# A new list of tasks, engines and addresses for four interleaved state-space and long-convolution layers on one core

## The chip, the cores and the metric

The kernel runs on one core of a Trainium2 chip. Time is device microseconds (us) of one execution of the whole program. Its engines are PE (matrix products; PEld is its weight load), DVE (vector), ACT (scalar functions), POOL (GpSimd) and SP (SyncE, which here only issues DMAs; SPq in the trace).

## What is computed

The input x has 2048 tokens of 640 channels. Two kinds of layer alternate, A, B, A, B, each added to x after a normalisation:

```python
x = x + _A_ref(_layernorm(x), Lambda_re, Lambda_im, B_re, B_im, C_re, C_im, log_dt, Dskip)
x = x + _B_ref(_layernorm(x), k, v, shift_k, ssm_k, ssm_D)
x = x + _A_ref(...)
x = x + _B_ref(...)
# _A_ref: Lam_bar = exp(dt*Lam); h[t] = Lam_bar*h[t-1] + x[t] @ B_bar.T   (complex, 640 states)
#         y = 2*Re(h @ C.T) + x*Dskip
# _B_ref: kv = conv4(k, shift_k) * v;  y = causal_conv(kv, ssm_k) + kv*ssm_D;  return q*y   (q is the normalised x)
```

Both A layers share their weights, and both B layers share y, which doesn't depend on x.

## The kernel before, in words

The work is cut into 912 named tasks. Each is added with S.add(name, engine, estimate, dependencies, function), and S.run (class Sched, L203) emits them in the order of one list of names, ORDER (L54). A name with /a, /d or /p chooses ACT, DVE or POOL for a task that may run on more than one. Each engine and SP's queue run their own tasks in the order of the list, and an engine stops at the first one whose inputs, buffer or PSUM bank are not ready. PLACE (L121) gives each buffer its address in one SBUF tile (arena, units of 64 bytes) or its PSUM bank (banks). The estimates and xt, a transfer time given to S.add for DMAs, are stored in the task and read by nothing in this program. Two buffers whose places overlap make the later one's first writer wait for the earlier one's last reader.

The tasks, by their names (N is a block of 128 channels, 0 to 4; c a chunk of 512 tokens, 0 to 3):

- yt_*: tables of sines and cosines for the transform in y (yt_sin on ACT, L857 to 859; yt_Ci and yt_Si are transposed copies by DMA, L872; yt_nsi, L876, writes the table NSi).
- kv_*N: kv_lkN loads k transposed (L1031), kv_lvN loads v (L1039), kv_mmN multiplies on PE (L1052), kv_evN multiplies by v on DVE (L1058). kv_dsN and kv_pdN prepare operands.
- a_*: weights of the A layers. a_ldB loads B, a_wl0j:c loads C transposed (L409, ten DMAs), a_wc (ACT, L413) and a_wm (DVE, L417) scale it, a_b0, a_b1 and a_w1 are products with copies a_b0e, a_b1e, a_w1e behind them, a_t2 ends the tables.
- yqN_*: the long convolution y of block N as a two-step transform. yqN_kl (L1133) loads ssm_k, yqN_vl (L1151) transposes kv from SBUF to SBUF by DMA. KA, KB, VA and VB (matmuls :m L1088, L1112 to 1117; copies out of PSUM :e, L254 on ACT or L256 on DVE) transform both, yqN_pw (L1165 to 1168) multiplies on DVE, IB (L1187, 1188) goes back, yqN_tt (L1200) transposes by DMA, IA (L1215) ends it and yqN_st (L1225) stores y in DRAM (ysd).
- xlc loads x, A1cc_xr loads it once more for the residual (L1313, L1317).
- Layers A1 and A2, chunk c: statistics (_ln_bn, L572, or _ln_sq, L545), _id (normalise), _tu (transpose by DMA, L629), _bq (L648) and _bp (L663, L665) on PE with copies _eq and _ev, then on DVE _ri (L680, 681, 684), the scan _sc (L692 to 697), the carry _cy (L708 to 710), _ro and _hx (L722), and on PE _cp:q (L745), with _xe:q (L753 on ACT, L755 or L757 on DVE) writing the new x and its sums.
- Layers B1 and B2, chunk c: B1lc, B2lc load y (L1328; they wait for all stores yqN_st), statistics, _u (normalise, L599 on ACT, L601 on DVE), _mm (L802), _m (L808 or L810). The last chunk of B2 goes token by token (_u L787, _m L791), and _st stores the output (L773).

The chain of one chunk is thus xl, _ln, _id, _tu, _bq, _bp, _ri, _sc, _ro, _hx, _cp, _xe, then B1 with y, then A2 and B2 in the same way. The scan of chunk c+1 waits for the carry of chunk c.

Of the kernel before, what the change touches and what calls it, by code (L numbers as in the profile page):

```python
# [66 lines left out]
    yq1_VA:m2 kv_mm2:0 kv_lv3 yq0_IB:e3/a a_wm04:0 yq1_VA:e2/a yq0_IB:m1 kv_ev2:0 a_wc02:0 yq0_IB:m4 yq1_VA:m1 a_wc04:1 yq0_IB:e1/d yq2_kl yq0_IB:m2
    yq1_VA:e1/a yq1_KB:m4 a_wm00:0 yq0_IB:e2/a yq1_VB:m1 a_wm02:0 yq0_IB:e4/a a_wl03:1 yq1_KB:e4/d a_wc00:1 yq1_VB:m0 a_wm04:1 yq1_VB:e1/a kv_mm3:0 yq2_vl
    a_wm00:1 yq1_VB:e0/a yq1_VB:m3 kv_ev3:0 a_wc02:1 yq1_VB:m2 yq1_VB:e3/a yq2_ka a_wm02:1 a_wl03:0 yq2_KA:m3 yq2_KA:m0 yq2_KA:e3/a kv_mm3:1 yq2_KA:e0/d
    yq0_tt yq1_VB:e2/a yq1_VB:m4 kv_ev3:1 yq2_KA:m2 yq1_VB:e4/a yq2_KA:m1 yq2_KA:e2/a yq1_pw yq2_VA:m3 yq2_KA:e1/a yq2_VA:m0 yq2_VA:e3/a yq2_KB:m2  # L70
    yq2_VA:e0/a yq2_VA:m2 kv_lv4 yq2_KB:e2/a yq2_KB:m0 yq2_VA:e2/a yq2_KB:m1 yq2_KB:e0/a xl0 yq0_IA:m0 a_wc03:0 kv_mm4:1 yq0_IA:e0/a a_wm03:0 yq2_KB:e1/a
    yq3_vl yq1_IB:m3 kv_ev4:1 a_wc03:1 yq2_KB:m4 yq1_IB:m4 yq1_IB:m2 yq2_KB:e4/a yq1_IB:e3/a a_wm03:1 yq1_IB:m1 yq3_kl A1c0_ln_bn:2/d yq1_IB:e4/a
    yq1_IB:e2/a yq0_IA:m1 yq2_VA:m1 A1c0_ln_bn:3/d yq1_IB:e1/a kv_mm4:0 A1c0_ln_bn:1/d yq0_IA:e1/a xl2 yq1_IB:m0 yq2_VA:e1/a A1c0_ln_bn:0/d yq2_KB:m3
    yq1_IB:e0/a kv_ev4:0 yq2_VB:m1 A1c0_ln_sd yq1_tt yq2_VB:m3 yq2_KB:e3/d yq2_VB:m0 yq2_VB:e1/a A1c0_ln_post yq2_VB:m2 yq3_ka yq2_VB:e0/d yq2_VB:e3/a
    yq3_KA:m3 yq2_VB:e2/a A1c0_id:0/d yq2_VB:m4 A1c0_id:3/d yq2_VB:e4/d A1c0_id:2/a yq3_KA:m2 yq2_pw yq3_KA:m1 A1c0_id:1/a yq3_KA:e3/a A1c0_tu yq3_KA:e1/a
    yq3_KA:e2/a yq3_KA:m0 yq3_KA:e0/a yq1_IA:m0 xl1 yq1_IA:m1 yq1_IA:e0/a yq3_KB:m1 yq1_IA:e1/a yq3_KB:m3 yq4_kl yq3_KB:e1/a yq3_VA:m3 A1c2_ln_bn:0/d
    yq2_IB:m3 yq3_VA:e3/a yq3_KB:e3/d yq2_IB:m2 yq2_IB:e3/a yq2_IB:m1 yq1_st A1c2_ln_bn:2/d yq2_IB:e2/a yq3_VA:m2 yq2_IB:m0 yq2_IB:e1/d yq3_VA:e2/a
    yq2_IB:m4 yq3_KB:m4 A1c2_ln_bn:3/d yq2_IB:e0/a yq0_st yq3_VA:m1 yq3_KB:m0 yq3_VA:e1/a yq2_IB:e4/d A1c0_bq:2 A1c2_ln_bn:1/d yq3_KB:e4/a yq3_KB:e0/a
    yq3_KB:m2 yq4_ka yq2_tt A1c1_ln_bn:2/d A1c0_eq:2/a yq3_VA:m0 yq4_KA:m0 A1c1_ln_bn:3/d A1c0_bp:2 yq3_VA:e0/a yq3_KB:e2/d A1c2_ln_sd yq3_VB:m2
    A1c0_ev:2/a A1c2_ln_post yq4_KA:e0/a A1c0_bq:1 A1c1_ln_bn:1/d yq3_VB:e2/a A1c2_id:0/d A1c1_ln_bn:0/d yq4_KA:m3 yq3_VB:m0 A1c2_id:2/d A1c0_eq:1/a  # L80
    yq4_KA:e3/d yq3_VB:m1 yq3_VB:e0/a A1c2_id:1/d yq3_VB:m4 yq3_VB:m3 A1c2_id:3/d A1c1_ln_sd yq3_VB:e4/d A1c2_tu A1c1_ln_post yq4_KA:m2 A1c0_bp:1
    yq3_VB:e3/a A1c1_id:3/d yq4_KA:e2/d yq3_VB:e1/a yq3_pw yq4_KA:m1 A1c0_bq:0 A1c0_ev:1/a xl3 yq4_KA:e1/a yq2_IA:m1 A1c0_xr A1c0_eq:0/a A1c2_bq:2
    yq2_IA:m0 A1c2_eq:2/a A1c0_bp:0 yq4_vl yq2_IA:e0/a yq2_IA:e1/a A1c1_id:0/a A1c1_id:1/d yq3_IB:m1 A1c1_id:2/d A1c0_ev:0/d A1c1_tu A1c2_bp:2 yq3_IB:e1/a
    A1c0_ri yq3_IB:m2 A1c2_ev:2/a yq3_IB:m3 yq3_IB:e2/a yq2_st yq3_IB:m0 yq3_IB:e3/a yq4_KB:m2 yq3_IB:e0/a yq4_KB:m3 yq4_KB:e2/a A1c0_sc A1c1_bq:0
    yq4_KB:e3/a A1c1_bq:1 A1c1_eq:0/a yq4_KB:m1 A1c1_eq:1/a A1c0_cy yq4_KB:m4 A1c0_ro A1c1_bq:2 yq4_KB:e1/a yq4_KB:m0 yq3_IB:m4 A1c1_bp:0 yq3_IB:e4/a
    yq4_KB:e0/a A1c3_ln_bn:3/a yq4_KB:e4/d yq3_tt A1c1_eq:2/d A1c2_bq:0 A1c3_ln_bn:1/d A1c1_ev:0/d yq4_VA:m3 A1c1_bp:2 A1c2_eq:0/a yq4_VA:e3/d yq4_VA:m0
    A1c3_ln_bn:2/d yq4_VA:m2 A1c1_bp:1 yq4_VA:e0/a A1c3_ln_bn:0/d A1c1_ev:2/a yq4_VA:e2/a A1c0_hx A1c3_ln_sd yq4_VA:m1 A1c2_bp:0 yq4_VA:e1/d A1c1_ev:1/d
    A1c3_ln_post yq4_VB:m3 A1c1_ri A1c2_bq:1 yq4_VB:e3/a A1c2_ev:0/a yq3_IA:m1 A1c2_eq:1/a yq4_VB:m4 yq4_VB:m2 yq4_VB:e4/a yq3_IA:e1/a A1c2_bp:1 A1c1_sc
    A1c1_xr yq4_VB:e2/a a_w10:4 A1c2_ev:1/a yq4_VB:m0 yq4_VB:m1 A1c0_cp:3 yq4_VB:e1/a yq4_VB:e0/d a_w1e0:4/a yq4_pw a_w10:1 A1c0_xe:3/a a_w10:3 a_w1e0:1/a
    a_w11:0 a_w1e0:3/a a_w10:0 a_w10:2 a_w1e1:0/a a_w11:2 a_w1e0:0/a a_w11:3 a_w1e0:2/a a_w11:4 a_w1e1:2/a a_w11:1 a_w1e1:4/a A1c0_cp:1 a_w1e1:3/a  # L90
# [191 lines left out]
def a_setup_tasks(S, nc, wp, St, consts, A_Lambda_re, A_Lambda_im, A_B_re, A_B_im, A_C_re, A_C_im, A_log_dt, A_Dskip, after_sin):  # L282
# [111 lines left out]
    t_bl = []  # L394
# [209 lines left out]
class ALayer:  # L604
# [6 lines left out]
    def chunk(self, c, src, sums_in, x_ready, resid, s_x, sums_out, s_src, reload):  # L611
        S, nc, aw, AT = self.S, self.nc, self.aw, self.AT
        small = self.small
        nm = f"{self.lname}c{c}"
# [5 lines left out]
        outs = []  # L620
# [750 lines left out]
```

## Time and profile before

| | us |
|---|---|
| median of 4 runs (lowest to highest) | 351.93 (350.55 to 354.01) |
| the profiled execution: its own time | 351.71 |
| its span, first to last instruction | 349.7 |
| DMA: moved in all | 41.70 MB in 111276 packets |

Spans in the trace start at its first instruction, so an event "at 130.67" is that far into the 349.7 us. A line of the time line gives start, length, engine, line of the code, operation, what it writes <- reads, the number of instructions merged, and in brackets how long the engine had been idle and what ended that. A "work ahead" of a task is the sum over one engine's tasks in front of it in the list, each from its start to the next one's start, less the idle time: what the engine has to do before it, without waits. The time at which the trace has the task, less its work ahead, is how long the engine had been idle by then.

### The profile page before, as it was taken

The numbers are of one execution on the slowest core, as the hardware profiler recorded it, in microseconds if no ns is written. First come the engines' busy times: TensorE is split into PE (matmuls) and PEld (weight loads), VectorE is DVE, ScalarE is ACT, GpSimd is POOL, SyncE is SP. The second block draws the span as 40 slices with busy tenths as digits, with TensorE's granted clock in tenths as the row PEclk, the third lists the DMA queues.
The fourth block names the chain that finished last, engine by engine and source line by source line (L and its number), as shares of the span: only waits on it lengthen the run. The fifth ranks groups of instructions, "written<-read, shape, count | busy, mean of one in ns | idle before, by whom it ended". The sixth has DMA issues, their size and how long they took to land.

```text
span 349.7 us, 9369 instructions
## 1 busy us (share of the span) xinstructions
PE 309.8 (89%) x4060; PEld 248.6 (71%) x4060; DVE 327.7 (94%) x455; ACT 254.6 (73%) x405; POOL 22.3 (6%) x58
## 2 busy tenths in 40 slices
PE   7687989779599989999999999999999999899900
PEld 7576878679598889896676786776877787566500
DVE  8999989988989999899999699999999999999996
ACT  5999999979997775655867669985975874007760
POOL 6567000000000000000000000000000000000000
PEclk9789999989899999999999999999999999999965
DMA  8999999999995990601049921703217400000033
GB/s 237 185 150 200 191 166 195 185 219 192 182 257 107 227 187 3 120 9 69 2 99 196 292 108 30 200 10 67 75 32 197 75 3 1 2 0 2 16 134 150
DMA packets 111276, 41.70 MB, mean 119 GB/s; under 512 B 104830, under 2 KB 106115, under 8 KB 111235
## 3 DMA queue, kind: packets, MB, share of 16 engines
q1 hardware_dynamic: 111088, 41.10, 57.2%
q8 instruction: 31, 0.51, 0.6%
q14 instruction: 11, 0.08, 0.1%
q10 hardware_dynamic: 146, 0.01, 0.0%
HBM read 17.38 MB, written 5.24 MB: 65 GB/s over the span
## 4 chain that ended last, share of the span: by engine, by line
PE 54%; DVE 27%; DMA 8%; ACT 7%; issue 2%; POOL 0%; DVEq 0%; POOLq 0%; ACTq 0%; SPq 0%
PE banks L745 18%; PE banks L663 10%; PE banks L648 9%; DMA arena<-arena 8%; DVE arena L697 5%; ACT arena L254 5%; DVE arena L680 4%; DVE arena L256 3%; DVE arena L757 2%; DVE arena L681 2%; DVE arena L810 2%; PE banks L1187 2%; PE banks L1188 2%; PE banks L665 2%; PE banks L1112 2%
## 5 line engine op out<-in xcount | busy, mean ns | idle before, releaser
L254 ACT ACTIVATE arena<-banks 128x1024 bf16<-128x1024 f32 (+3 forms) x150 | 129.1, 927 | 37.5 <-PE banks L665 10.3
L745 PE MATMUL banks<-arena 128*128 128x128 bf16 (+1 forms) x800 | 100.9, 283 | 1.3 <-DVE arena L681 1.3
L745 PEld LDWEIGHTS <-arena 128*128 128x128 bf16 x800 | 60.5, 98 | 41.3 <-DVE arena L681 1.4
L663 PE MATMUL banks<-arena 128*128 128x256 bf16 x400 | 53.3, 273 | 0.0
L648 PE MATMUL banks<-arena 128*128 128x256 bf16 x400 | 46.0, 273 | 1.2 <-ACT arena L254 1.2
L680 DVE TENSOR_TENSOR arena<-arena 128x5160 bf16<-128x5160 bf16 x16 | 45.5, 2842 | 0.3
L256 DVE CAST arena<-banks 128x1024 bf16<-128x1024 f32 (+4 forms) x43 | 41.7, 981 | 4.0 <-issue 1.2
L697 DVE TENSOR_TENSOR_SCAN arena<-arena 128x1290 bf16<-128x1290 f32 x16 | 44.7, 2833 | 0.3
L648 PEld LDWEIGHTS <-arena 128*128 128x128 bf16 x400 | 38.5, 98 | 5.7 <-DMA arena<-arena 1.4
L663 PEld LDWEIGHTS <-arena 128*128 128x128 bf16 x400 | 38.5, 98 | 4.8
L545 ACT ACTIVATE junk<-arena,nmean 128x640 bf16<-128x640 f32 x48 | 39.6, 825 | 1.1
L599 ACT ACTIVATE arena<-arena,nmr,rstd 128x640 bf16<-128x640 f32 (+1 forms) x37 | 32.5, 914 | 8.7 <-DVE nmr L558 8.5
L1112 PE MATMUL banks<-arena 128*128 128x128 bf16 x170 | 36.1, 225 | 1.4 <-ACT arena L254 0.9
L1115 PE MATMUL banks<-arena 128*128 128x128 bf16 x170 | 36.4, 224 | 0.0
L1114 PE MATMUL banks<-arena 128*128 128x128 bf16 x150 | 33.6, 224 | 0.0
L1117 PE MATMUL banks<-arena 128*128 128x128 bf16 x150 | 33.4, 223 | 0.0
L681 DVE TENSOR_TENSOR arena<-arena 128x2580 bf16<-128x2580 bf16 x16 | 24.1, 1503 | 0.6
L665 PE MATMUL banks<-arena,ident_bf 128*128 128x256 bf16 x80 | 21.8, 272 | 0.0
L540 ACT ACTIVATE nmean<-sums 128x4 f32<-128x4 f32 (+1 forms) x15 | 3.0, 199 | 24.7 <-DVE arena L757 17.8
L1187 PE MATMUL banks<-arena 128*128 128x128 bf16 x160 | 20.8, 227 | 0.2 <-ACT arena L254 0.2
L1188 PE MATMUL banks<-arena 128*128 128x128 bf16 x160 | 20.7, 227 | 0.0
L1088 PEld LDWEIGHTS <-arena 64*128 64x128 bf16 x320 | 10.1, 97 | 11.9 <-issue 7.1
(195 smaller groups left out, 508.5 us busy)
## 6 DMA issues: line engine op xcount, KB each, us to landing
arena<-in_A_x_dram SPq DMA_DIRECT2D x8, 640.0 KB, 6.8
arena<-ysd SPq DMA_DIRECT2D x8, 640.0 KB, 5.2
arena<-in_B_ssm_k_dram SPq DMA_DIRECT2D x5, 512.0 KB
arena<-in_B_v_dram SPq DMA_DIRECT2D x5, 512.0 KB, 4.9
ysd<-arena SPq DMA_DIRECT2D x5, 512.0 KB, 6.8
out_dram<-arena SPq DMA_DIRECT2D x8, 320.0 KB, 2.2
arena<-in_A_B_re_dram SPq DMA_DIRECT2D x1, 800.0 KB, 4.8
arena<-in_A_B_im_dram SPq DMA_DIRECT2D x1, 800.0 KB, 6.6
```

The source lines that it names most:

```text
L254: nc.scalar.activation(out, in_, ACT.Copy)
L256: nc.vector.tensor_copy(out, in_)
L545: nc.scalar.activation(small.junk, src(q), ACT.Square, bias=st["nmean"][:, i:i + 1], scale=1.0, accum_out=st["ssq"][:, i:i + 1])
L648: nc.tensor.matmul(pq[:, jj, c2, :], lhsT=bt0[:, c2, k, j * P:(j + 1) * P], rhs=uT[:, 2:4, k, :], start=(k == 0), stop=(k == NJ - 1))
L663: nc.tensor.matmul(pb[:, jj, c2, :], lhsT=bt1[:, c2, j, k, :], rhs=uT[:, 0:2, k, :], start=(k == 0), stop=False)
L680: nc.vector.tensor_tensor(tt, gs[:, :, None].to_broadcast([P, 2, 2, n]), by_pairs(w["tab"].get().rearrange("p i j b -> p (i j b)"), n), AL ...
L697: nc.vector.tensor_tensor_scan(gv, rt, gv, 0.0, ALU.mult, ALU.add)
L745: nc.tensor.matmul(pc[:, o0:o1], lhsT=lh, rhs=rh, start=(n == 0), stop=(n == len(ops) - 1))
L1112: nc.tensor.matmul(ps[:, g, 0, :], lhsT=T["Cf"].get()[:, q, :], rhs=are, start=True, stop=single)
L1114: nc.tensor.matmul(ps[:, g, 0, :], lhsT=T["Sf"].get()[:, q, :], rhs=A[:, 2 * q + 1, :], start=False, stop=True)
L1115: nc.tensor.matmul(ps[:, g, 1, :], lhsT=T["NSf"].get()[:, q, :], rhs=are, start=True, stop=single)
L1117: nc.tensor.matmul(ps[:, g, 1, :], lhsT=T["Cf"].get()[:, q, :], rhs=A[:, 2 * q + 1, :], start=False, stop=True)
```

## The change

ORDER and PLACE are replaced as a whole; both hold the same 912 tasks and the same buffers. 67 tasks with a choice change between ACT and DVE (34 to DVE, 33 to ACT) and five between DVE and POOL. The order changes on every engine, by less than 20 places of the list for most tasks; further go, among others, yq2_kl and yq2_ka (112 places earlier), yq4_vl (73 earlier), yq1_vl (58 earlier), kv_lk3 (78 later), kv_lk4 (62 later), yq1_st (135 later), yq2_st (47 later), A1c0_xr (75 later), a_wl02:1 (156 later), B2l1 (145 earlier). Besides, some of the xt numbers are new. Some of its lines (ORDER and PLACE have 64 and 42 lines on each side):

```diff
 ORDER = """
...
-    yq1_VA:m2 kv_mm2:0 kv_lv3 yq0_IB:e3/a a_wm04:0 yq1_VA:e2/a yq0_IB:m1 kv_ev2:0 a_wc02:0 yq0_IB:m4 yq1_VA:m1 a_wc04:1 yq0_IB:e1/d yq2_kl yq0_IB:m2
...
-    yq3_VB:e3/a A1c1_id:3/d yq4_KA:e2/d yq3_VB:e1/a yq3_pw yq4_KA:m1 A1c0_bq:0 A1c0_ev:1/a xl3 yq4_KA:e1/a yq2_IA:m1 A1c0_xr A1c0_eq:0/a A1c2_bq:2
-    yq2_IA:m0 A1c2_eq:2/a A1c0_bp:0 yq4_vl yq2_IA:e0/a yq2_IA:e1/a A1c1_id:0/a A1c1_id:1/d yq3_IB:m1 A1c1_id:2/d A1c0_ev:0/d A1c1_tu A1c2_bp:2 yq3_IB:e1/a
...
-    a_w1e1:1/a A1c3_id:1/d A1c3_id:3/a A1c1_cy A1c1_ro yq4_IB:m3 yq3_IA:m0 yq4_IB:e3/a A1c0_cp:0 yq3_IA:e0/a A1c3_id:0/a A1c0_xe:1/d yq3_st A1c2_ri
...
+    yq0_vl kv_mm1:0 kv_ev1:1 yq0_KB:m3 kv_ev1:0 a_b01:1 yq0_KB:m4 yq2_kl a_lamd a_b01:0 yq0_KB:e4/a a_b0e1:1/a yq0_KB:e3/d yq1_vl a_b10:1 a_b0e1:0/a
...
+    yq1_VA:m3 kv_mm2:1 yq1_VA:e3/a yt_nsi a_wl03:0 yq1_VA:e0/a a_wm00:0 yq0_IB:m3 a_wl04:1 kv_ev2:1 a_b1e1:1/a yq0_IB:m0 a_wc02:0 kv_mm2:0 kv_lk3 a_t2
+    yq0_IB:e3/a yq0_IB:e0/d yq1_VA:m2 kv_ev2:0 yq1_VA:e2/a yq0_IB:m1 kv_lv3 a_wc04:0 yq0_IB:m4 yq1_VA:m1 yq0_IB:m2 yq0_IB:e4/d yq1_VA:e1/a yq0_IB:e1/d
...
+    yq3_KB:e1/a A1c2_ln_bn:3/d yq2_IB:m3 yq3_VA:e3/a yq3_KB:e3/d yq2_IB:m2 yq2_IB:e3/a yq2_IB:m1 A1c2_ln_bn:1/d yq2_IB:e2/a yq4_vl yq3_VA:m2 yq2_IB:m0
...
+    yq2_IA:m0 A1c1_tu A1c0_eq:0/a yq4_KB:m4 yq2_IA:m1 A1c2_bq:2 yq2_IA:e0/a A1c3_ln_bn:3/a A1c0_bp:0 A1c2_eq:2/d yq4_KB:e4/d yq2_IA:e1/d A1c2_bp:2
...
+    A1c1_hx yq4_IB:m3 yq4_IB:e1/a yq4_IB:m0 yq4_IB:e3/d yq4_IB:m2 yq4_IB:e0/a yq4_IB:m4 A1c0_cp:2 yq4_IB:e2/a yq4_IB:e4/d A1c2_ri yq4_tt A1c1_cp:3
...
 PLACE = {
...
-    3176, "x2:2": 1565, "x2:3": 444, "A1c2_u": 288, "A1c2_uT": 2326, "A1c2_g": 1284, "A1c2_q": 524, "A1c2_t": 1565, "A1c2_t2": 1571, "xb3": 2429, "xr3":
...
+    "x2:1": 3038, "x2:2": 40, "x2:3": 2638, "A1c2_u": 507, "A1c2_uT": 2326, "A1c2_g": 1284, "A1c2_q": 524, "A1c2_t": 873, "A1c2_t2": 1571, "xb3": 2406,
...
-        t_bl.append(S.add(f"a_ldB{i}", "sp", 0.5, [], e_ld, xt=2.2, uses=[s_B[i]]))
+        t_bl.append(S.add(f"a_ldB{i}", "sp", 0.5, [], e_ld, xt=2.6, uses=[s_B[i]]))
...
-        H["t_tt"] = S.add(f"yq{qd}_tt", "sp", 4.9, eI, e_tt, xt=5.5, uses=[s_TT, s_T])
+        H["t_tt"] = S.add(f"yq{qd}_tt", "sp", 4.9, eI, e_tt, xt=4.4, uses=[s_TT, s_T])
```

The other new xt numbers are those of a_wl (0.95 to 1.2), _tu (3.3 to 3.4), kv_lk (2.7 to 2.5), kv_lv (2.4 to 2.7), yqN_vl (2.6 to 2.75) and yqN_st (2.2 to 1.9).

## The prediction

> **What bounds the kernel now.** I read the page's busy shares first, then the busy time by stage, then the chain that ended last, and last the time line of the engines around each wait.
>
> ```profile
> PE 309.8 (89%) x4060; PEld 248.6 (71%) x4060; DVE 327.7 (94%) x455; ACT 254.6 (73%) x405; POOL 22.3 (6%) x58
> ```
>
> VectorE (DVE) works 327.7 of 349.7 us, so no order can bring more than some 22 us, and of these 2.1 lie before its first table instruction and 3.3 behind its last (the final store). The stages differ, though (columns: stretch, length, busy PE, PEld, DVE, ACT, POOL, clock, DMA share, GB/s):
>
> ```profile
> 40.00:50.00 10.00, 8.59 (x149) 8.22 (x146) 9.43 (x8) 9.90 (x15) 0.00 (x0) 1.00 1.05 183
> 60.00:70.00 10.00, 8.03 (x245) 7.00 (x244) 9.68 (x9) 9.91 (x13) 0.00 (x0) 1.00 1.09 181
> 120.00:130.00 10.00, 9.47 (x142) 8.89 (x138) 9.53 (x9) 8.67 (x11) 0.00 (x0) 1.00 1.09 204
> 150.00:160.00 10.00, 10.00 (x132) 9.15 (x131) 9.79 (x10) 6.09 (x7) 0.00 (x0) 1.00 0.22 67
> 300.00:310.00 10.00, 10.00 (x81) 5.91 (x80) 9.86 (x10) 0.00 (x0) 0.00 (x0) 1.00 0.01 2
> ```
>
> To about 115 us ACT and DVE share the copies out of PSUM, both are over 90% busy, and the DMA share is about 1. From 130 us PE has no gap to 299, and DVE has 9.8 of 10. The chain of waits says the same: PE carries it to 268 us, then DVE to the end.
>
> ```profile
> 126.16 4.48 ACT arena L254 x5
> 130.67 4.54 PE banks L648 x40
> ...
> 259.05 9.00 PE banks L745 x75
> 268.07 1.58 DVE arena L757 x4
> ```
>
> So the end moves by what is saved before PE becomes gapless at 130.67, and by what changes in DVE's tail. At 130.67 PE starts A1c1_bq:0 after 1.19 us of waiting, and its weight load names a DMA (PEld L648, 1.4 us). SyncE's queue (SPq) shows why:
>
> ```profile
> 116.86 0.37 SPq L1317 DMA_DIRECT2D arena<-in_A_x_dram  x1
> 117.27 6.08 SPq L1151 DMA_TRANSPOSE arena<-arena  x1
> 123.87 3.54 SPq L629 DMA_TRANSPOSE arena<-arena  x1
> ```
>
> L1151 is yq4_vl, which nobody reads before 143 us, and L629 is A1c1_tu, which PE is waiting for. It was queued behind. DVE's larger waits are few:
>
> ```profile
> 52.42 1.23 DVE L1058 TENSOR_TENSOR arena<-banks,arena 128x1024 bf16<-128x1024 f32 x1 [1.00 <-DMA arena<-in_B_v_dram]
> ...
> 61.16 1.23 DVE L1058 TENSOR_TENSOR arena<-banks,arena 128x1024 bf16<-128x1024 f32 x1
> ...
> 196.92 0.82 DVE L755 TENSOR_SCALAR_CACHE_REDUCE arena<-banks 128x640 f32<-128x640 f32 x1 [2.72 <-PE banks L745]
> ...
> 202.58 1.49 DVE L802 TENSOR_TENSOR arena<-arena 128x2560 bf16<-128x2560 bf16 x1 [0.72 <-ACT std L550]
> ```
>
> **The change, part by part.** The xt numbers are read by nothing that runs; only ORDER and PLACE reach the chip. The sum is made against the profiled execution's own 351.7 us (span 349.7; the median of the four runs is 351.93, so 0.2 above it).
>
> *Choice of engine.* 34 tasks go from ACT to DVE, 33 from DVE to ACT, 5 between DVE and POOL. Busy time per piece, DVE / ACT, from the groups of instructions: 1024 columns 1.21 / 0.98, 512 0.69 / 0.59, 640 0.79 / 0.66, 256 0.41 / 0.40, normalising f32 0.56 / 0.87, bf16 0.41 / 0.92. To DVE go 12 of 1024, 7 of 512, 1 of 640, 3 of 256, 8 f32, 1 bf16 and 2 W1 copies: 14.5+4.8+0.8+1.2+4.5+0.4+1.6 = 27.8 us. Off it go 11, 2, 6, 0, 9, 3, one state copy (0.83) and one pair of statistics (1.07): 13.3+1.4+4.7+5.0+1.2+0.8+1.1 = 27.5 us. The five small ones take 0.2 off. DVE: 0.0 us. ACT by the same count: +29.6-27.0 = about +2.5 us. From 130 us on ACT is idle a third of the time and hides it. Before, it is not hidden: the work listed on ACT up to the last copy that yq3_pw needs (yq3_VB:e3) adds up to 101.6 us before and 104.6 after. That copy ended at 113.8, so ACT had been idle 12.2 by then. With all of that idle time kept it ends 3.0 later and yq3_pw (114.7) about 2.1 later; but 2.7 of it, from 95 us on, are waits for PE that more work fills, and 0.74 at 50.7 was a wait for yq1_vl, which now goes out earlier. I take 0; ends 0 and +2.1.
>
> *SyncE's queue to 100 us.* Its issues stand back to back (65.06 to 70.39, 70.49 to 71.02, and so on), so I add their start-to-start times. Ahead of yq0_tt there are 2.7 us less (kv_lk4 goes behind it), which PE and ACT, that both wait for it at 73.7 (2.29 and 1.28 us), partly get; but PE now meets that wait ahead of yq2_VA:m2, KB:m1 and KB:m4, which it had done before: 0. yq1_vl goes ahead of yt_Ci: PE's 1.36 us at 50.3 and ACT's 0.74 go. Next in line there is DVE's copy rate. kv_lk3 and kv_lv3 move behind all ten a_wl loads, and yq2_kl far ahead of both: the queue ahead of kv_lv3 is 59.1 us after the first issue (0.7), against 53.9 now. Issued at 59.8 and with the 4.9 that kv_lv3 took from 54.64 to its landing at 59.55, it lands at 64.7, while DVE wants it at 61.2 (kv_ev3:0). Behind that on DVE stand a_wm02:1, kv_ev3:1 and yq1_pw. The lower end is no wait, since part of the summed times is queue pressure (xl0 took 1.93 to issue, xl3 the same form 0.37). So -1.7 (0.74 and the 1.00 of kv_lv2) to +3.5. I take 0: the gain at 50 to 52 us against a landing near 62.
>
> The Trainium skill, "Perfetto Trace Analysis", What "DMA-bound" means, says that an issuing track that is solid DMA slices shows descriptor generation, not data movement. The two rows of one form, 1.93 and 0.37, disagree: the longer holds 1.56 us of something else. By the rule the shortest row of each form would be its price, kv_lv3 would go out as soon as its buffer is free, and the sum would lose the +3.5; by the rows it keeps it.
>
> *yq4_vl ahead of yq0_st and yq2_tt, yq1_st and yq2_st late.* A1c1_tu then stands behind xl3 alone, and its inputs (ACT's A1c1_id:0, after yq3_VB:e3 at about 114) are ready near 116: issue 3.5, landing some 2 later, 122, well ahead of 128.8. PE's 1.19 goes; ends -1.9 (A1c1_bq:0 also stands 0.7 us of work earlier in PE's list) and 0 (a copy on ACT is named for the same wait). The early yq4_vl puts 6.6 us into the queue ahead of yq2_tt, and yq1_st (2.4) leaves it: issued near 106.8 instead of 102.6 and landing 8.5 later (yq1_tt: 83.85 to 92.33), at 115.3. What covers it is that PE reads it first at 118 (yq2_IA); if that cover of 2.7 us is gone, PE waits for it as it does now for A1c1_tu. I take -1.2.
>
> *130 to 205 us.* PE's list is nearly as it was: the work ahead of yq3_pw, yq4_pw, A1c1_ro and B1c0_mm is 95.5, 142.3, 150.7 and 180.8 us in both. DVE's differs: 4.1 us less ahead of A1c1_ri and yq4_pw, so DVE comes early and waits for PE (yq3_IB:e2, yq4_VA:e0, yq4_VB:e1). That costs nothing as long as PE sets the pace. A1c2_ri is put behind yq4_IB:e4, and its new place A1c2_t (873) overlaps the table yNSi (880), which yq4_IB:m4 reads. PE ends that at 179.3; A1c2_ri started at 176.1. It becomes 3.6 late; behind it on DVE stand A1c2_sc and the whole of A2. The cover is the 2.72 and 0.72 at 196.9 and 202.6, which PE and the store of y caused and which a later DVE no longer meets. In front of B1l0 A1c2_xr (1.92 of issue) is gone, B1l0 took 6.3 to land and B2l2 alone 4.1: up to -2.2 for B1c0_mm. I take 0 for this stage, ends -2.2 and +3.4 (the cover gone).
>
> *Tail.* Behind the last A2 output on DVE 12.1 us of work stood, now 11.3: -0.7, ends -0.8 and 0 (nothing there speaks for a gain or loss beyond it, as PE's total is the same 309.8).
>
> Sum: 0 + 0 + 0 - 1.2 + 0 - 0.7 = -1.9; 351.7 - 1.9 = **349.8 us**.
>
> **The rivals.**
> - *All transfer waits go.* For it: three of the larger waits name a DMA. To -1.9 add -1.7 (50 to 52 us) and -2.2 (B1l0): 345.9. Against: from 130 us PE is gapless, and an earlier B1l0 alone does not move PE.
> - *A1c2_ri late (slower).* DVE works 163.9 us from A1c2_ri to its end (164.2 before) and was idle 6.1 there. Started 3.6 later, with the 3.4 of waits not returned: 351.7 + 3.6 - 0.3 = 355.0. It decides from the point where A1c2_ri starts after 179.5 (176.1 + 3.4). Against: DVE's waits at 196.9 and 202.6 had other causes than DVE.
> - *kv_lv3 late.* It lands at 64.7 and DVE, PE behind kv_mm3:0 and ACT all lose 3.5: 351.7 + 3.5 = 355.2. For it: DVE and ACT are both over 96% busy there. Against: issue times shrink where less is queued.
> - *Nothing moves.* PE's list is the same to a few tasks, so the 1.2 may be met by the copy on ACT: 351 to 352. It lies within the likeliest one's own range.
>
> **How the numbers follow.** Likeliest case (with nothing moving) 0.47, its own range 348 to 353; transfer waits gone 0.28; A1c2_ri 0.14; kv_lv3 0.11. A measurement here tells about 1% from no change: under 348.4 or over 355.4. Faster: the 0.28 and 0.03 from the likeliest one's edge, 0.31. Slower: most of the two late cases, which add in part to each other, 0.22. The rest 0.47. The range takes in 345.9 and 355.2 with a little of their spread: 345.5 to 356.5.
>
> **What would show it.** Right: A1c1_bq:0 (L648 near 129) without a wait; yq4_vl issued near 96; kv_ev3:0 (L1058 near 61) waiting under 1 us; A1c2_ri (L680) at 177 to 179, and no wait of 2.7 near 195. Wrong: DVE waits of over 2 us for in_B_v near 62; A1c2_ri after 179.5 with waits behind it as before; yq3_pw (L1165 near 115) after 116, which would make ACT's 2.5 us the price.

## The result, and the profile after

The new list takes 353.06 us (median of 33 executions, 350.84 to 356.17), the old one 351.88 (54 executions, 349.40 to 354.70): ratio 1.0035, interval 1.0019 to 1.0050. It is some 1.2 us slower, where 2 us faster was forecast. (Of one kernel below, h_after_before, three of twelve executions lay over 1.5% above its fastest; its time and ratio leave them out.) The profiled execution has a span of 352.4 us. Busy times first, then the same stretches as before:

```profile
PE 311.8 (88%) x4060; PEld 250.2 (71%) x4060; DVE 327.7 (93%) x452; ACT 257.8 (73%) x411; POOL 24.9 (7%) x59
```

```profile
40.00:50.00 10.00, 9.46 (x167) 9.19 (x164) 8.10 (x6) 10.00 (x15) 0.00 (x0) 1.00 1.09 173
60.00:70.00 10.00, 8.02 (x241) 6.97 (x239) 9.24 (x11) 10.00 (x13) 4.56 (x8) 1.00 1.21 191
...
120.00:130.00 10.00, 10.00 (x136) 9.27 (x135) 8.97 (x8) 6.70 (x13) 0.00 (x0) 1.00 0.74 139
150.00:160.00 10.00, 10.00 (x128) 8.97 (x126) 9.80 (x8) 6.02 (x8) 0.00 (x0) 1.00 0.88 210
300.00:310.00 10.00, 10.00 (x88) 6.12 (x86) 9.90 (x13) 0.00 (x0) 0.00 (x0) 1.00 0.01 2
```

DVE is as busy as before to a tenth (327.7), ACT 3.2 us more, and PE has no gap any more between 120 and 130 us. The waits that the forecast named, in the time line, on SyncE's queue and on DVE:

```profile
100.35 2.13 SPq L1151 DMA_TRANSPOSE arena<-arena  x1
...
118.84 0.58 SPq L1313 DMA_DIRECT2D arena<-in_A_x_dram  x1
120.89 4.43 SPq L629 DMA_TRANSPOSE arena<-arena  x1
```

```profile
63.17 1.22 DVE L1058 TENSOR_TENSOR arena<-banks,arena 128x1024 bf16<-128x1024 f32 x1 [0.65 <-issue]
...
182.22 0.42 DVE L256 CAST arena<-banks 128x256 bf16<-128x256 f32 x1 [0.56 <-PE banks L1188]
182.71 2.85 DVE L680 TENSOR_TENSOR arena<-arena 128x5160 bf16<-128x5160 bf16 x1
...
194.21 0.81 DVE L755 TENSOR_SCALAR_CACHE_REDUCE arena<-banks 128x640 f32<-128x640 f32 x1
...
203.84 1.48 DVE L802 TENSOR_TENSOR arena<-arena 128x2560 bf16<-128x2560 bf16 x1
```

yq4_vl is out of A1c1_tu's way; kv_ev3:0 waits 0.65 us; A1c2_ri (L680 at 182.7; its first instruction, at 182.6, came at 176.1 before) is 6.5 late, where 3.6 was worked out; and the waits of 2.72 and 0.72 ahead of L755 (the first of the four A1c1_xe) and L802 are gone. Nearly all of that was foreseen, and the sum is still wrong. One table shows in which stretches. It cuts the span of each profiled kernel at the start of three tasks: yq3_pw on DVE, A1c1_bq:0 on PE, A2c3_ri on DVE (from the trace; each column counts from the one before it; us; the kernels are those of the next section):

| kernel | to yq3_pw | to A1c1_bq:0 | to A2c3_ri | to the end |
|---|---|---|---|---|
| before | 114.71 | 15.95 | 170.69 | 48.29 |
| b_vl | 115.83 | 15.47 | 170.89 | 48.29 |
| b_relief | 115.70 | 15.51 | 170.56 | 48.30 |
| b_id | 115.68 | 14.38 | 170.67 | 48.30 |
| b_id_tt | 114.82 | 14.38 | 170.65 | 48.32 |
| b_b0 | 118.11 | 15.66 | 170.66 | 48.30 |
| after | 117.49 | 14.84 | 171.72 | 48.31 |
| a_mid | 114.34 | 14.84 | 171.70 | 48.27 |
| a_relief | 114.98 | 14.84 | 172.20 | 48.27 |
| a_place | 115.16 | 14.84 | 171.72 | 48.25 |
| a_noid | 114.33 | 14.84 | 171.73 | 48.68 |
| a_b0 | 115.49 | 14.84 | 171.73 | 48.66 |

The last three columns hardly scatter, so one profile of each is enough there. The second is 0.6 to 1.1 us shorter with the new list than with the old one where that keeps a wait (the gain that was foreseen), the third 0.8 to 1.2 longer (1.3 to 1.6 in a_relief), the last the same but for 0.4 in two kernels. The first scatters by 3 us for one and the same list: six profiles of the new list's first part (after, a_mid, a_relief, a_place, a_late, a_tail) have a mean of 115.4, four of the old one's (before, b_vl, b_relief, b_late) 115.3. The 117.49 of the first profile after, from which one would read a loss of 2.8 us, is an outlier.

The third column ends at a task of DVE, and DVE waits for PE. A cut on PE itself is sharper. A2c2_bp:2 is the last task of PE before A2c3_ri that has the same PE tasks ahead of it in both lists. Its end comes 152.3 to 152.4 us behind A1c1_bq:0 in all six kernels with the old list and 153.2 in all six with the new. PE is busy without a gap up to there (before, b_relief, after, a_relief; columns as in the forecast, from A1c1_bq:0 to the end of A2c2_bp:2):

```profile
130.67:283.02 152.35, 152.35 (x1472) 116.13 (x1473) 144.77 (x176) 110.54 (x200) 0.00 (x0) 1.00 0.39 91
131.21:283.54 152.33, 152.33 (x1472) 116.12 (x1473) 141.74 (x171) 113.76 (x206) 0.00 (x0) 1.00 0.38 91
132.33:285.53 153.20, 153.20 (x1487) 116.74 (x1485) 149.28 (x174) 112.80 (x202) 0.00 (x0) 1.00 0.40 101
129.82:283.02 153.20, 153.20 (x1487) 116.72 (x1485) 143.16 (x167) 117.35 (x211) 0.00 (x0) 1.00 0.40 102
```

DVE's work in it differs by 3 us (b_relief) and 6 us (a_relief), and PE's time stays the same to 0.02 us. So PE sets the pace from A1c1_bq:0 to A2c2_bp:2, and the new list has 0.9 us more of PE's work there. That 0.9 is complete early: the last matmul of A1c1_bp comes 17.03 us behind A1c1_bq:0 in after and 16.16 in before.

### The profile page after: what moved, and what is told of

Its sections match the earlier page's. It is cut to its first block, busy times and chain, and to the rows that moved or that the text cites. A ratio compares the mean times of both kernels' runs of the same rounds, so it can differ in the third digit from the quotient of the medians.

```text
span 352.4 us, 9379 instructions
## 1 busy us (share of the span) xinstructions
PE 311.8 (88%) x4060; PEld 250.2 (71%) x4060; DVE 327.7 (93%) x452; ACT 257.8 (73%) x411; POOL 24.9 (7%) x59
## 4 chain that ended last, share of the span: by engine, by line
PE 54%; DVE 31%; ACT 6%; issue 3%; SPq 2%; DMA 1%; ACTq 1%; DVEq 0%
PE banks L745 15%; PE banks L663 8%; PE banks L648 8%; DVE arena L680 6%; DVE arena L697 5%; DVE arena L757 3%; PE banks L1112 3%; DVE arena L810 2%; PE banks L1115 2%; DVE arena L681 2%; PE banks L1188 2%; PE banks L1187 2%; PE banks L1117 2%; PE banks L1114 2%; PE banks L1088 2%
## 5 line engine op out<-in xcount | busy, mean ns | idle before, releaser
L256 DVE CAST arena<-banks 128x1024 bf16<-128x1024 f32 (+4 forms) x47 | 43.7, 941 | 11.7 <-PE banks L1117 3.9
L648 PE MATMUL banks<-arena 128*128 128x256 bf16 x400 | 46.3, 273 | 0.0
L680 DVE TENSOR_TENSOR arena<-arena 128x5160 bf16<-128x5160 bf16 x16 | 45.5, 2843 | 0.3
L648 PEld LDWEIGHTS <-arena 128*128 128x128 bf16 x400 | 38.5, 98 | 4.4
L599 ACT ACTIVATE arena<-arena,nmr,rstd 128x640 bf16<-128x640 f32 (+1 forms) x40 | 34.7, 911 | 9.1 <-DVE nmr L558 9.1
L753 ACT ACTIVATE arena<-banks 128x640 f32<-128x640 f32 x14 | 9.8, 699 | 13.0 <-PE banks L745 12.8
```

The source lines that it names most:

```text
L256: nc.vector.tensor_copy(out, in_)
L648: nc.tensor.matmul(pq[:, jj, c2, :], lhsT=bt0[:, c2, k, j * P:(j + 1) * P], rhs=uT[:, 2:4, k, :], start=(k == 0), stop=(k == NJ - 1))
L680: nc.vector.tensor_tensor(tt, gs[:, :, None].to_broadcast([P, 2, 2, n]), by_pairs(w["tab"].get().rearrange("p i j b -> p (i j b)"), n), AL ...
```

## The experiments

Kernels named a_ are after with an edit, b_ before with an edit. In all of them the code stands one line higher (L647 is L648).

**Halves.** Each joins one list to A1c0_ln_post (85 us, both hold the same tasks by then) with the other behind it.

```diff
 ORDER: tasks of before up to A1c0_ln_post, then of after   (h_before_after; h_after_before the reverse)
 PLACE: 153 buffers (73) elsewhere than in after
```

> The list and the choices of before up to A1c0_ln_post (85 us; both lists hold the same tasks ahead of it), then those of after. The places had to be found anew (153 buffers elsewhere than in after); nothing is left out. Theory 'lost early': the new list loses 2.1 us by A1c0_ln_post (85.42 to 87.56 in the two profiles) and wins about 0.9 behind it (the end is 1.2 later by the medians). Then this kernel takes 351.9 - 0.9 = 351.0. Rival 'lost late': the early delay is covered by waits that the first list has anyway, and the loss is made behind 118 us (A1c2_ri 6.5 late, 2.3 to 2.7 us in layer A2). Then it takes 353.1, as after.

> The other half: the list and the choices of after up to A1c0_ln_post, then those of before, in places found anew (73 buffers elsewhere than in after). Nothing is left out. 'Lost early': 351.9 + 2.1 = 354.0, and A1c0_ln_post near 87.5. 'Lost late': 351.9, with A1c0_ln_post near 87.5 all the same, and DVE's waits of 2.72 and 0.72 us at 196.9 and 202.6 shorter by what is late.

Measured 356.10 (1.0144, 1.0109 to 1.0179) and 353.78 (1.0054, 1.0023 to 1.0085). The first is slower than either whole list, the second slower than before and not told from after, so the halves don't add up. The first lost 1.3 us between yq3_pw and A1c2_ri (66.5 against 65.2 in after) and 0.9 in the tail, which no whole list loses; whether the seam or the new places cost that wasn't tried. Inconclusive.

**The choice of engine.**

```diff
-a_b0e1:1/a a_b0e1:0/a yq0_VB:e2/a yq0_VB:e0/d ...   (a_choice: 22 ahead of yq3_pw, as before)
+a_b0e1:1/d a_b0e1:0/d yq0_VB:e2/d yq0_VB:e0/a ...
-yq4_IB:e3/d yq4_IA:e0/d B1c1_u:0/d ...   (a_late: 33 behind A1c1_ri, as before; b_late: the reverse in before)
+yq4_IB:e3/a yq4_IA:e0/a B1c1_u:0/a ...
```

> After, with the choice between ACT and DVE as before in the 22 copies and normalisations ahead of yq3_pw that differ (12 back to DVE, 10 back to ACT); order and places of after. Nothing is left out. Theory 'ACT is the price': yq0_pw waited 1.34 us for an ACT copy (yq0_VB:e4) and yq1_pw came 2.44 late, since ACT has 3 us more to do by then: yq0_pw back near 43.2, yq1_pw near 66.5, and a time of 351. Rival 'PE and the transfers': DVE's waits at 86.4, 89.3 and 101.4 (1.62, 1.34, 1.20) name PE, whose own waits come from kv_lk4 and from a stop in the middle of kv_mm4:0; the choice of engine moves nothing there: 353, and the waits stay.

> After, with the choices between ACT and DVE that before has, in the 33 tasks behind A1c1_ri (152 us) that differ; order and places of after. Nothing is left out. Theory 'DVE behind A1c1_ri': from there to the end DVE works 192.4 us in after and 188.7 in before, and is idle 7.7 and 9.8; the new choices took 3.7 us of DVE's work out of the stage where it waits for PE and put it where it has no idle time. The 33 tasks take 4.4 us off DVE; if some 2 of them come back as waits, as before has them, the time is 353.1 - 2.4 = 350.7, and A1c1_ri to A2c3_ri shrinks from 151.8 towards 150.2. Rival 'PE sets it' (PE is gapless from 97 to 323 us): DVE only waits more, 353.1, and A1c1_ri to A2c3_ri stays at 151.8.

> The other way round: before, with the choices of after in the same 33 tasks behind A1c1_ri; order and places of before. Nothing is left out. 'DVE behind A1c1_ri': 4.4 us more for DVE, some 2 of it in its waits (2.72 and 0.72 us at 196.9 and 202.6): 351.8 + 2.4 = 354.2. 'PE sets it': 351.8.

Measured 355.22 (1.0109, 1.0077 to 1.0142), 357.12 (1.0146, 1.0106 to 1.0186) and 364.60 (1.0358, 1.0327 to 1.0390). No theory foresaw this: taking the old choices into the new list makes it slower, early or late, and b_late loses 12.4 us. DVE in the time line of b_late shows where:

```profile
199.59 0.83 DVE L754 TENSOR_SCALAR_CACHE_REDUCE arena<-banks 128x640 f32<-128x640 f32 x1 [2.11 <-PE banks L744]
...
206.72 1.49 DVE L801 TENSOR_TENSOR arena<-arena 128x2560 bf16<-128x2560 bf16 x1 [3.06 <-ACT arena L598]
...
222.87 0.07 DVE L683 MEMSET arena<- 128x10 uint32 x1 [3.13 <-ACT arena L253]
...
296.28 0.69 DVE L255 CAST arena<-banks 128x512 bf16<-128x512 f32 x1 [4.23 <-PE banks L664]
```

DVE stands at its next task in the list, twice for ACT itself (a normalisation, L598, and a copy, L253), twice for PE; PE in turn had stood 0.99 us at 196.1 and 3.88 at 290.4 for a copy on DVE (L255). So the waits go round between the three engines. These choices cost time in both orders that they weren't made for, and a sum of so many pieces at so much each doesn't give that.

**Is DVE the bound behind 150 us?** By DVE's rows it seemed so: the new list has 3.7 us more DVE work behind A1c1_ri (192.4 against 188.7) and 2.1 less idle time there.

```diff
-yq4_VB:e0/d A1c0_xe:1/d A1c3_eq:1/d A2c0_eq:2/d A2c2_ev:2/d   (b_relief)
+yq4_VB:e0/a A1c0_xe:1/a A1c3_eq:1/a A2c0_eq:2/a A2c2_ev:2/a
-a_w1e1:1/d a_w1e1:4/d yq4_IB:e3/d yq4_IB:e4/d yq4_IA:e0/d A1c3_eq:2/d A2c1_eq:2/d A2c1_ev:2/d A2c2_eq:2/d   (a_relief: all to /a)
-yq4_VB:e1/d a_w1e1:1/d a_w1e1:4/d A1c3_id:2/d yq4_IB:e3/d yq4_IB:e4/d   (a_mid: to /a; yq4_VB:e0, A1c0_xe:1, A1c3_id:1 to /d)
```

> Before, with five copies behind A1c1_ri given from DVE to ACT: yq4_VB:e0, A1c0_xe:1, A1c3_eq:1, A2c0_eq:2, A2c2_ev:2, 4.6 us of DVE's work (1.20, 0.82, 1.22, 0.69, 0.69), some 3.9 us on ACT, which is idle a third of the time there. Nothing is left out. 'DVE behind A1c1_ri': up to 4.6 less; if half comes back as waits for PE, as the five larger waits of before show it can, 351.8 - 2.3 = 349.5. 'PE sets it': 351.8, with the 4.6 us as new DVE waits for PE.

> After, with nine copies behind A1c1_ri given from DVE to ACT, where before has them too: a_w1e1:1 and :4, yq4_IB:e3 and :e4, yq4_IA:e0, A1c3_eq:2, A2c1_eq:2, A2c1_ev:2, A2c2_eq:2, 7.3 us of DVE's work; the normalisations stay as in after. Nothing is left out. Theory 'DVE has become the bound': in after DVE is idle only 4.0 us from A1c1_ri to A2c3_ri (6.1 in before) and the tail behind A2c3_ri is 48.3 us in all kernels, so copies taken from it move A2c3_ri: from 151.8 behind A1c1_ri to 150 or less, and the time to 351.5 or less. Rival 'PE and DVE bind together': as in the same trial on the kernel before (4.6 us given away, nothing won), the time becomes DVE waits for PE and ACT: 353.1.

> After, with the choices of before only between A1c1_ri and A1c2_ri (nine tasks, 2.6 us off DVE in net). Nothing is left out. A1c2_ri came 30.3 us behind A1c1_ri in after and 24.9 in before. Theory 'DVE work ahead of A1c2_ri is the price of the late stage': A1c2_ri about 26.8 us behind A1c1_ri, and A2c3_ri and the end 1.5 us earlier: 351.6. Rival 'covered': A1c2_ri is as early, the gain is met again by DVE's wait for PE or for the normalisation on ACT ahead of B1c0_mm and B1c1_mm, and the time is 353.1.

Measured: b_relief 352.09 (0.9994, 0.9967 to 1.0021), a_relief 353.04 (1.0031, 1.0008 to 1.0053), a_mid 352.05 (1.0022, 0.9991 to 1.0052). Nothing is won. DVE in the time line of a_mid:

```profile
178.88 2.85 DVE L679 TENSOR_TENSOR arena<-arena 128x5160 bf16<-128x5160 bf16 x1 [2.89 <-PE banks L1187]
...
190.47 0.81 DVE L754 TENSOR_SCALAR_CACHE_REDUCE arena<-banks 128x640 f32<-128x640 f32 x1
...
200.68 1.48 DVE L801 TENSOR_TENSOR arena<-arena 128x2560 bf16<-128x2560 bf16 x1
```

a_mid doesn't test the cover of A1c2_ri: DVE gets there earlier, but its first product (L679) waits 2.89 us for PE, which reads the table NSi in the same place (yq4_IB:m4), and starts 49.7 us behind A1c1_bq:0, in after 50.4. What does show the cover is after against before: A1c2_ri comes 50.4 us behind A1c1_bq:0 instead of 45.5, and B1c0_mm (L802; L801 in a_mid) 71.5 instead of 71.9. So A1c2_ri being 4.9 us later was fully covered. That DVE isn't what sets the pace is shown by PE's time in the last section, which b_relief and a_relief leave as it was.

**What made PE wait at A1c1_bq:0?**

```diff
-A1c0_bp:0 yq4_vl yq2_IA:e0/a ... A1c1_tu A1c2_bp:2   (b_vl)
+A1c0_bp:0 yq2_IA:e0/a ... A1c1_tu yq4_vl A1c2_bp:2
-yq3_pw ... A1c0_ev:1/a ... yq4_vl ... A1c1_id:0/a A1c1_id:1/d ... A1c1_id:2/d ... A1c1_tu   (b_id)
+A1c1_id:1/d A1c1_id:2/d yq3_pw ... A1c1_id:0/a A1c0_ev:1/a ... A1c1_tu yq4_vl
-A1c1_id:2/d A1c1_id:1/d A1c1_id:3/a yq3_pw A1c1_id:0/a ... A1c0_ev:1/a   (a_noid)
+A1c1_id:3/a yq3_pw A1c1_id:1/d A1c1_id:2/d ... A1c0_ev:1/a A1c1_id:0/a
```

> Before, with one task moved: yq4_vl behind A1c1_tu, which it had held up in SyncE's queue. Nothing is left out. As predicted, PE's wait of 1.19 us at A1c1_bq:0 goes; if that wait sets the end, 351.9 - 1.2 = 350.7. Rival 'covered': DVE is the slower engine there (9.8 of 10 us busy), and PE's next wait takes its place: 351.9, with A1c1_bq:0 earlier and yq4_pw where it was (162.96).

> Before, with four tasks moved: A1c1_id:1 and A1c1_id:2 ahead of yq3_pw on DVE, A1c1_id:0 ahead of A1c0_ev:1 on ACT, A1c1_tu ahead of yq4_vl in SyncE's queue. Nothing is left out. The earlier trial moved yq4_vl alone, and A1c1_tu went out no earlier (124.4 against 123.9), because A1c1_id:0 to :2 were ready only at 123.2. Theory 'the normalisations held up A1c1_tu': it now goes out near 118, PE's wait at A1c1_bq:0 goes, yq3_pw is up to 0.8 later; if PE sets the end there, 351.8 - 0.8 = 351.0. Rival: DVE's 0.8 us in front of yq3_pw takes the gain back, 351.8.

> After, with A1c1_id:1 and :2 behind yq3_pw on DVE and A1c1_id:0 behind A1c0_ev:1 on ACT, close to where before has them. Nothing is left out. Theory 'the order of A1c1_id is what the new list wins': A1c1_tu goes out some 4 us later, PE waits about 1 us at A1c1_bq:0, and it takes 354. Rival: yq3_pw is 0.8 us earlier and PE has other work in front of A1c1_bq:0; 353.1.

Measured: b_vl 352.06 (0.9996, 0.9967 to 1.0024), b_id 349.82 (0.9953, 0.9926 to 0.9981), a_noid 352.15 (1.0024, 0.9996 to 1.0053). The time line's rows of SyncE's queue, and of PE or its weight load, in b_vl, then b_id, then a_noid:

```profile
124.44 3.01 SPq L628 DMA_TRANSPOSE arena<-arena  x1
127.51 3.29 SPq L1150 DMA_TRANSPOSE arena<-arena  x1
...
131.29 1.75 PEld L647 LDWEIGHTS <-arena 128*128 128x128 bf16 x17 [0.88 <-DMA arena<-arena]
```

```profile
118.56 6.12 SPq L628 DMA_TRANSPOSE arena<-arena  x1
124.74 3.02 SPq L1150 DMA_TRANSPOSE arena<-arena  x1
...
130.06 3.11 PE L647 MATMUL banks<-arena 128*128 128x256 bf16 x27
```

```profile
122.59 3.00 SPq L628 DMA_TRANSPOSE arena<-arena  x1
...
129.17 2.35 PE L647 MATMUL banks<-arena 128*128 128x256 bf16 x20
```

In b_vl, A1c1_tu (L628) goes out no earlier although yq4_vl (L1150) is behind it: A1c1_id:0 to :2 stand behind yq3_pw and are ready at 124.3 (123.2 in before). So yq4_vl alone did not hold it up, as the forecast had said; the normalisations stood in the way too. But a_noid has them nearly as late (122.5) and PE doesn't wait: there the transfer has SyncE's queue to itself and lands 4.9 us after its issue, while in b_vl, with yq4_vl right behind, PE gets it 6.9 us after. In the old list, then, moving yq4_vl alone leaves 0.9 us of the wait, and b_id, which moves the normalisations ahead as well, has none. (The normalisations alone weren't tried there.) b_id is faster than before, by 0.5%, and than after, by 0.9%: in the old list, the wait of 1.19 us is worth about what the forecast put it at (-1.2), and it reaches the end.

**The first 115 us.**

```diff
 a_sp:     SyncE's first 32 DMAs in the order of before; 39 buffers moved
 a_place:  38 buffers of after moved, list and choices unchanged
-a_b0e1:1/a a_b0e1:0/a   (a_b0: to /d; a_b0_kb4: yq0_KB:e4/a to /d as well; b_b0: the reverse of a_b0 in before)
-a_wl03:0 yq2_KA:m3 ... yq0_tt   (b_id_tt: in b_id)
+yq0_tt a_wl03:0 yq2_KA:m3 ...
```

> After, with SyncE's first 32 DMAs (to xl0, 74 us) in the order of before; choices and the order on PE, DVE, ACT and POOL as in after; 39 buffers had to be moved for it. Nothing is left out. Theory 'the queue to 100 us costs': yq0_ka back from 13.5 to 12.3, PE without its waits of 2.13 at 14.0 (L1088) and 1.45 at 74.7 (kv_lk4), kv_ev3:0 without its 0.65; A1c0_ln_post back from 87.6 to about 85.5, and the end 1 to 2 us earlier, 351.5. Rival 'covered': those waits are taken over by the next one (ACT's copies for yq0_pw, PE for yq2_KB:e3), A1c0_ln_post moves by less than 1 us, 353.1.

376.30 (1.0684, 1.0657 to 1.0711), but for a reason of the edit: yq2_kl went out 25 us later (51.1), close to where before has it; yq2_ka, which reads it, stayed at its early place in the list, and DVE stood there (time line):

```profile
58.26 0.23 DVE L1137 TENSOR_TENSOR arena<-arena,kd 128x16 bf16<-128x16 bf16 x1 [22.89 <-DMA arena<-in_B_ssm_k_dram]
```

It tells nothing on the queue, but one thing on the rest: A1c0_ln_post comes 20.4 us later and the span is 21.3 longer. What the first part loses is not made up.

> After, with the same list and choices and 38 buffers in other places, chosen so that fewer first writers stand close behind the last reader of an overlapping buffer. Nothing is left out. Theory 'the places cost': A1c2_ri no longer waits for yq4_IB:m4 through the table NSi, and the time falls by up to 1 us, 352.1. Rival 'the list sets it': 353.1, with the same DVE waits at 86, 89, 101, 129 and 132 us. It is also a second look at the first 118 us of the new list.

353.06 (1.0022, 0.9989 to 1.0055): the places cost nothing that can be seen.

> After, with the two copies a_b0e1:1 and a_b0e1:0 on DVE, as before has them. Nothing is left out. In after they stand on ACT behind a_t1 (24.5 to 30.5 us), and PE waits 1.93 us for them at 30.8 (a_b10:1); from 32.5 PE runs at half clock for 3.4 us. Theory 'ACT's copies make PE idle, and the idle time halves its clock': the wait falls under 1.2, no half clock between 30 and 37 us, mean granted clock nearer to 0.960, and the time up to 1 us less: 352.1. Rival: DVE, with 1.6 us more, is late for yq0_KB:e3 and yq0_VA, PE waits for those, and it stays at 353.1.

> The other way round: before, with a_b0e1:1 and a_b0e1:0 given to ACT. Nothing is left out. Theory: PE waits about 2 us for them behind a_t1 (25.6 to 31.7), a stretch of half clock appears between 31 and 37 us, yq0_pw and all behind it come later by up to 1 us: 352.8. Rival: DVE's 1.6 us less make it early by as much, and it is 351.9 or less.

> After, with three copies on DVE in place of ACT: a_b0e1:1, a_b0e1:0 and yq0_KB:e4. Nothing is left out. Theory 'the bank behind a_t1': PE's wait of 1.9 us at 31 to 32 falls below 1, and no half clock between 30 and 40 us. If that stretch sets the end, yq0_pw comes 1 us earlier or more and the time falls to 352; if DVE and ACT pace the first 115 us, yq3_pw stays near 115.3, the mean of seven profiles of the new list, and the time at 352.8.

a_b0 352.76 (1.0036, 1.0013 to 1.0059), b_b0 354.36 (1.0081, 1.0052 to 1.0109), a_b0_kb4 354.42 (1.0096, 1.0063 to 1.0128). In the old list the two copies on ACT do what was expected, PE's wait and the half clock behind it, and the price is 2.7 us (time line, then busy time by stretch):

```profile
32.91 0.27 PE L446 MATMUL banks<-arena 128*128 128x128 bf16 x1 [4.03 <-ACT arena L253]
```

```profile
32.00:39.00 7.00, 5.95 (x67) 5.38 (x67) 3.41 (x13) 4.52 (x7) 1.43 (x5) 0.52 1.18 191
```

In the new list neither edit removes the wait. PE's a_b10:1 waits for another task, a_lamd (L364) on DVE, which ends at 31.25 in the time line of a_b0_kb4:

```profile
29.10 2.15 DVE L364 TENSOR_TENSOR arena<-ident_bf,s_lam 128x1920 bf16<-128x1920 bf16 x1
...
31.64 0.22 PE L446 MATMUL banks<-arena 128*128 128x128 bf16 x1 [1.96 <-DVE arena L255]
```

In after it ends at 30.43 and a_b10:1 starts at 30.78; in a_b0, 31.67 and 32.01. The copy named as the releaser only ended last. That a_lamd is the cause is read from these times and wasn't tried.

> The kernel b_id (before, with A1c1_id:0 to :2 and A1c1_tu earlier, 349.8), with one more move: yq0_tt ahead of a_wl03:0 in SyncE's queue. Nothing is left out. yq0_tt would go out near 63.2 instead of 65.1; in before PE waits 2.29 us for it at 73.7 and then runs at half clock for 3.4 us (75.2 to 78.6). Theory 'PE's idle time ahead of 97 us and the half clock behind it set the end': the wait falls to about 0.4, the half clock between 72 and 80 us goes, and the time falls by 1 to 2 us: 348.5. Rival: DVE (96% busy there) and ACT set the pace, and PE only waits later: 349.8.

350.24 (0.9963, 0.9940 to 0.9986), against 349.82 for b_id: PE's wait for yq0_tt is 0.72, against 1.94 in b_id (2.29 in before), and no gain can be seen. A wait of PE ahead of 97 us need not cost its length; the 4.03 of b_b0 did cost 2.7.

**The tail.**

```diff
-A2c3_ri A2c1_cp:0 A2c1_xe:3 A2c1_xe:2 B2c0_mm A2c2_cp:3 A2c1_xe:0 A2c3_sc ... A2c3_ro
+A2c3_ri A2c1_cp:0 A2c1_xe:3 A2c3_sc A2c1_xe:2 B2c0_mm A2c2_cp:3 A2c1_xe:0 A2c3_ro ...
```

> After, with A2c3_sc behind A2c1_xe:3 on DVE (three tasks and 3.9 us earlier) and A2c3_ro behind A2c1_xe:0. Nothing is left out. Theory 'PE's waits for A2c3_ro are on the path': the 1.97 and 0.46 us at 323 to 327 go and the time falls by 1 to 2.4: 351. Rival 'DVE alone sets the tail': it has no idle time from A2c3_ri to its last instruction, and that stretch takes 48.3 us in every kernel so far; 353, at most 0.4 less where the wait had drawn a stretch of half clock at 322.

355.86 (1.0099, 1.0063 to 1.0134): both wrong. PE waits longer, since A2c1_xe:2 and :0, which free its banks, are now behind the scan, and DVE waits 1.17 and 2.16 us in the tail, where other kernels have 0.3 at most (time line of a_tail):

```profile
314.04 4.43 PE L744 MATMUL banks<-arena 128*128 128x512 bf16 x10 [3.50 <-DVE arena L756]
...
322.83 0.82 DVE L756 SCALAR_TENSOR_TENSOR arena<-banks,arena 128x640 f32<-128x640 f32 x1 [1.17 <-PE banks L744]
...
325.83 0.82 DVE L756 SCALAR_TENSOR_TENSOR arena<-banks,arena 128x640 f32<-128x640 f32 x1 [2.16 <-PE banks L744]
```

## Why the prediction was wrong, step by step

- *Choice of engine, 0.* DVE's total was right to a tenth and ACT's +2.5 came out as +3.2. yq3_pw is at 115.4 in the mean of both lists, so ACT's upper end of +2.1 didn't come. But the step took the choices for a sum of prices; a_choice, a_late and b_late show that such a sum misses what a choice costs in another order.
- *SyncE's queue to 100 us, 0.* kv_ev3:0 waits 0.65, within what was named; the rival of 3.5 us didn't come (kv_lv3 went out at 57.4, not at 59.8). The waits at 50 to 52 us went, as foreseen, but others came (PE's 1.45 at 74.7 for a load). No experiment isolated this step.
- *yq4_vl, -1.2.* This is the step that failed. PE's wait went, and yq3_pw to A1c1_bq:0 is 0.6 to 1.1 us shorter. The cause was half right (the normalisations stood in the way too). But the gain ends there: from yq3_pw to the end of A2c2_bp:2 the new list takes 168.0 us in all six kernels, the old one 167.8 to 168.3 where it keeps a wait and 166.7 where b_id takes it out. Without its waits the old list has 167.1 us of PE's work there, the new one 168.0. So when yq3_pw starts, PE has 0.9 us more still to do, and the wait that was won pays for that; the term came to about 0. Of the 0.9, 0.7 shows at A1c1_bq:0: it stands 0.7 us earlier in PE's list, which the forecast booked as a possible gain (the end of -1.9), but yq4_KB:m2 (0.89 us) went behind it and yq4_KB:m4 (0.22) ahead, and PE has to do that work afterwards. The other 0.2 has no single task: it is spread over rows where PE changes from one task to another.
- *130 to 205 us, 0.* Right for DVE: B1c0_mm is 71.5 us behind A1c1_bq:0 (71.3 to 72.3 in six kernels with the old list), and A1c2_ri, 4.9 us later, was covered. On PE the 0.9 us just named is already there by the end of A1c1_bp. DVE, which has its own waits in the old list, doesn't show it at B1c0_mm. The rival of 355.0 met its condition (182.6, past 179.5), but not its second half, waits that stay as before.
- *205 to 300 us: no term.* From B1c0_mm to A2c3_ri it is 100.2 us, with the old list 98.6 to 99.4 in the six kernels of the table, which looks like the loss. PE's cut shows that it isn't: PE brings the 0.9 us from 150 us, and in this stretch DVE runs into it. Of the +1.0 between A1c1_bq:0 and A2c3_ri the last 0.2 lies behind A2c2_bp:2 (18.5 us to A2c3_ri against 18.3). "PE's list is nearly as it was" was checked by the work ahead of four tasks, the last at 203 us; what PE has left to do at the marker of the gain, A1c1_bq:0, wasn't counted.
- *Tail, -0.7.* Measured 0.0 (48.31 against 48.29 us from A2c3_ri to the end, DVE's work 44.64 and 44.65). The term failed as well: the 0.8 us taken from behind the last output had gone ahead of it, into the same stretch that DVE fills alone. In two profiles (a_noid, a_b0) it is 0.4 longer, with PE at half clock behind its new wait (time line of after):

```profile
323.48 3.17 PE L745 MATMUL banks<-arena 128*128 128x512 bf16 x25 [1.97 <-DVE arena L681]
```

- The sum of what the profiles show is 0 (to yq3_pw, in the mean) - 0.6 to - 1.1 + 1.0 + 0 to 0.4: between -0.1 and +0.8. The timed executions say +1.2 (0.7 to 1.8). So 0.4 to 1.3 us of the loss are in no stretch that repeats. They may lie in the first 115 us of executions that weren't profiled; that stays open. What speaks for it: PE's wait of 2.13 us at 14.0 (for yq0_ka, whose load goes out behind kv_lk0 too) is new, and the one of 1.93 at 30.8 was 1.17; and over all timed executions the new list has a mean granted clock of 0.9554, the old one 0.9595. Over 352 us that would be 1.4 us as an upper estimate; among executions of one and the same list, so much less clock goes with 0.5 to 0.6 us more span.
- *The rivals.* "Nothing moves" (351 to 352) was nearest in kind: one wait gone, its worth handed on, though to PE's own list and not to the copy on ACT. "All transfer waits go" falls with the result: the waits at 50 to 52 us went, B1c0_mm moved by 0.4 us at most, and the time isn't 345.9.

## What to carry to other kernels

A new order moves work past every marker that one measures at: count each engine's work ahead of and behind the marker, and book as gain only what disappears, not what changes sides. Put the markers on the engine that sets the pace: a marker on another engine shows a loss where that engine runs into it, not where it arises. Give every stretch of the program its own term, also where the list looks unchanged. Where one execution differs from the next by as much as the effect, compare stretches that repeat to 0.1 us, and don't read a cause from the one that scatters.

## What the runs showed of the hardware

PE can stop in the middle of a loop without a wait that the profile shows. In after, within kv_mm4:0, it stood still from 80.9 to 83.1; the chain calls it issue (PE waited for nothing that the profile shows), and between 80 and 82 the DMA view has one packet on an instruction queue (0.02 MB), while the DMA share reads 2.93. Then came 3.4 us at half clock. The chain, then the busy time by stretches (columns as in the forecast):

```profile
80.88 2.23 issue
```

```profile
81.00:82.00 1.00, 0.00 (x0) 0.00 (x0) 0.97 (x4) 1.00 (x2) 0.00 (x0) 1.00 2.93 134
82.00:83.00 1.00, 0.00 (x0) 0.00 (x0) 0.76 (x3) 0.27 (x1) 0.00 (x0) 1.00 0.37 16
83.00:84.00 1.00, 0.89 (x21) 0.84 (x22) 0.42 (x1) 0.00 (x0) 0.00 (x0) 0.85 0.60 134
84.00:87.00 3.00, 3.00 (x31) 3.00 (x30) 1.38 (x2) 2.33 (x3) 0.00 (x0) 0.50 0.52 114
```

That the load is what stopped PE is inferred from the two standing together, not shown; shorter stops, of 0.6 to 1.1 us and with no other releaser either, stand in the same task in seven other profiles (b_id 1.11, a_place 0.62). The half clock comes in stretches of 3.4 us or a multiple, behind an idle PE: behind the 2.29 us at 73.7 in before (75.2 to 78.6), and not behind the 0.72 us that b_id_tt leaves of it. A wait near 2 us brings it in some executions and not in others: none behind 1.97 us at 323.5 in after, 3.4 us of it (321.6 to 325.0) behind 1.98 at 320.3 in a_noid, none behind 1.94 at 73.9 in b_id.
